# Moving the down-projection in front of the third score unit of its slot

## The chip, the cores and the metric

The kernel runs on one core of a Trainium2 chip. The metric is device time in microseconds (us) of one execution, taken as the median over several runs. The engines of the core run their own instruction lists side by side and wait for each other by semaphores: TensorE (PE, with its weight loads shown as PEld), VectorE (DVE), ScalarE (ACT), GpSimd (POOL) and SyncE (SP, which here only starts DMAs).

## The reference

Two parts follow each other. The first is an attention in which keys and values are a pooled and projected image; the second adds, to each row, the output of two out of eight small adapters.

```
kv_pool = kv averaged over 4 x 4 patches          # 4 images of 384 x 32 -> 768 rows of 128
k = v = kv_pool @ w_sr
s = q @ k.T / sqrt(128);  a = softmax(s);  x = a @ v        # 4 x 12288 queries
logits = x @ w_gate;  the two largest of 8 get softmax weights w, the rest 0
out = x + sum over e of w[e] * (x @ A[e]) @ B[e]            # A: 128 -> 16, B: 16 -> 128
```

The eight adapters together are one 128 x 128 matrix A (the down-projection) and one 128 x 128 matrix B (the up-projection); the weights w scale the 128 hidden values in between, 16 for each adapter.

## The kernel before

The 49152 query rows are cut into 96 chunks of 512. A loop runs over slots, and in each slot several chunks are at different stages:

- `unit()` takes the next score unit from a list: for one chunk and two of the six blocks of 128 keys, `scores` makes two matmuls of 512 columns into a PSUM tile `sg` (pool `ps_s`, two buffers), and ACT writes their exponential to `em`. Three units make a chunk, and there are three `unit()` calls in a slot.
- `attend(k, s)` makes six matmuls with `em` as weights into `acc`; four of them (s = 0 to 3) make the attention output of a chunk. `normalize` divides on DVE (`rinv`, then `xn`).
- `top` and `route` find the two adapters (DVE's MAX8 and then POOL), `tanhs` and `gates` make the weights `gw` (one ACT instruction and two on POOL).
- `transposes(x, h, engine)` turns, with TensorE, `xn` of one chunk and the gated hidden values `hg` of another into one PSUM tile `tt_ps`, which DVE copies to `tts` in SBUF. Some chunks have their `hg` turned by a DMA instead (`turn_h_dma`, to a tile `ht`), and the chunks from number 68 to 89 have both turned by DMA.
- `down(x)` makes four matmuls with the turned `xn` as weights into `h_ps`; `gate(x)` multiplies `h_ps` by `gw` on DVE to `hg` (or `hs`). `up(u)` makes four matmuls into `d_ps`; `finish(u)` adds `xn` on DVE (`osb`) and stores.

`tt_ps`, `h_ps`, `d_ps` and the tiles for preparing keys and values of the next image (`kpT_ps`, `v_ps`, `kfT_ps`) all come from the pool `ps_m` with two buffers, in the order in which they are asked for. `keep` fixes the program order on each engine, so the order in which the lines stand is the order in which each engine takes its instructions.

From slot 8 on the loop at line 588 writes the order. In a common slot it is: first `unit()` (line 600), `tanhs`, `normalize`, `transposes`, second `unit()` (653), `up` and `finish` (654 to 656), `attend(…, 0)` (663), `top` and `route` (665), then from slot 13 on the third `unit()` (667) and in slots 8 to 12 `attend(…, 1)` in its place (670), then `down` (673) and `gate` (675 or 681), then the rest of the `attend` calls. Slots whose chunks are all turned by DMA leave the loop earlier, at line 636. Where a piece of the preparation of the next image is due, it stands between `gate` and the last `attend` calls (line 684).

Of the kernel before, what the change touches and what calls it, by code (L numbers as in the profile page):

```python
# [20 lines left out]
def kernel(  # L21
# [47 lines left out]
    def mm(*a, **k):  # L69
        return keep(nc.tensor.matmul(*a, **k))  # L70

    def mtile(shape, dtype=FP32, name="mb"):
        return ps_m.tile(shape, dtype, tag="mb", name=name)
# [12 lines left out]
    def load_qT(g):  # L86
        if g < B * NG - GC:
            t = qpool.tile([P, GT], BF16, tag="qT", name="qT")
        else:
            if "q" not in spare:  # L90
                spare["q"] = kvpool.tile([P, 4, 2, 4 * C], FP32, tag="kvr", name="qTs")
            t = spare["q"][:, g % GC].rearrange("p x c -> p (x c)").bitcast(BF16)
        keep(nc.sync.dma_start(t.rearrange("c (i r) -> c i r", r=16), q_bf[g], transpose=True))
        qT[g] = t
# [228 lines left out]
    def normalize(k):  # L323
        ri = rpool.tile([P, S], FP32, tag="rinv", name="rinv")
        keep(nc.vector.reciprocal(ri, acc[k][:, :, VC]))  # L325
        k0, m = first[k], k - first[k]
        if m == 0:
            xg[k0] = ring[len(xg) % len(ring)]
        x = xg[k0][:, m]
        keep(nc.vector.tensor_tensor(x[:, :, 0:VC], acc[k][:, :, 0:VC],  # L330
                                     ri.unsqueeze(2).broadcast_to([P, S, VC]), op=ALU.mult))
        xn[k] = x
# [12 lines left out]
    def top(k):  # L345
        k0, m = first[k], k - first[k]
        if m == 0:
            srt[k0] = rpool.tile([P, GC, S, 8], FP32, tag="srt", name="srt")
        for s in range(S):
            keep(nc.vector.max(srt[k0][:, m, s], xn[k][:, s, C:C + E]))  # L350
# [3 lines left out]
    def route(k0):  # L354
        n = size[k0] * S
        eng = nc.gpsimd if k0 > 1 else nc.vector
        lg = xg[k0].rearrange("p m s c -> p (m s) c")[:, 0:n, C:C + E]
        so = srt[k0].rearrange("p m s e -> p (m s) e")[:, 0:n]

        def over(i):  # L360
            d = rpool.tile([P, GC * S, 8], FP32, tag=f"over{i}", name=f"over{i}")[:, 0:n]
            keep(eng.tensor_tensor(  # L362
                d, lg, so[:, :, i].unsqueeze(2).broadcast_to([P, n, 8]), op=ALU.subtract))
            return d

        arg, mask = over(0), over(1)
        keep(eng.tensor_tensor(arg, arg, mask, op=ALU.add))
        keep(eng.tensor_scalar(mask, mask, 0.0, None, op0=ALU.is_ge))  # L368


        later.append(lambda: gates(k0, n, eng, arg, mask))
# [40 lines left out]
    def narrow(k, t):  # L412
        keep(nc.gpsimd.tensor_copy(strip(t, 0)[:, 0], xn[k][:, :, 0:C]))
# [13 lines left out]
    def down(k):  # L427
        hp[k] = mtile([P, S, P], name="h_ps")
        for s in range(S):
            mm(hp[k][:, s], xT[k][:, s], a_bf, start=(s == 0), stop=(s == S - 1))  # L430
# [10 lines left out]
    def up(k):  # L441
        dp[k] = mtile([P, S, C], name="d_ps")
        for s in range(S):
            mm(dp[k][:, s], hgT[k][:, s], b_bf, start=(s == 0), stop=(s == S - 1))
# [30 lines left out]
    def unit(k=None, r=None):  # L475
        k, r = units.pop(0 if k is None else units.index((k, r)))
        scores(k, r)
# [26 lines left out]
    def begin(k, queries=True):  # L504
        nonlocal sums, rest
        b, i = divmod(k, NB)
        g = k // GC
        if k in loads and queries:
            load_qT(loads[k])
        if k in casts:  # L510
            cast_q(4 + casts.index(k))
        if k in rows_at:
            load_kv(*rows_at[k], None)
        if i == 0 and 0 < b < B - 1:
            rest = prepare(b + 1, nc.gpsimd)[1]
        if k == 3:
            sums, rest = prepare(1, nc.gpsimd)
            sums = sum(sums, [])
        if 3 <= k < 15:
            load_kv(1, (k - 3) // 4, (k - 3) % 4, None)  # L520
        if k == 7:
            for _ in range(2):
                sums.pop(0)()

    def tanhs():
        while later:
            later.pop(0)()
# [60 lines left out]
    for k in range(k1, NCHUNK):  # L588
        b, i = divmod(k, NB)
        ka = att.get(k, [])  # L590
        kx = enter.get(k, [])
        begin(k, False)

        def after_norm(kn):
            top(kn)
            if kn == first[kn] + size[kn] - 1:
                route(first[kn])

        kn = [n for n in att.get(k - 1, []) if normed[n] == k]
        unit()  # L600
        if k in loads and not any(x_ in by_queue for x_ in kx):
            load_qT(loads[k])
        ku = ku + late_up.pop(k, [])
        if kx and not kd and all(x_ in by_dma for x_ in kx):
            down(kx[0])
            todo = []
            for n in kn:
                normalize(n)
                if n in by_dma:
                    narrow(n, k)  # L610
                    todo = [(xT, n)]
            tanhs()
            for h_ in kh:
                if h_ not in by_dma:
                    transposes(None, h_, nc.vector)
            unit()
            gate(kx[0], strip(k, 0)[:, 1])
            todo.append((hgT, kx[0]))
            if len(kx) == 1:
                turn_dma(k, *todo)  # L620
            for u_ in ku:
                up(u_)
                finish(u_)
            attend(ka[0], 0)
            attend(ka[0], 1)
            unit()
            for n in kn:
                after_norm(n)
            attend(ka[0], 2)
            for x_ in kx[1:]:  # L630
                down(x_)
                gate(x_, strip(k, 0)[:, 0])
                turn_dma(k, (hgT, x_), *todo)
            attend(ka[0], 3)
            kh, ku = kx, [c for c in kh if c not in by_queue]
            continue
        tanhs()
        for x_ in kd:
            down(x_)
        for n in kn:  # L640
            normalize(n)
            if n in by_dma:
                narrow(n, k)
                turn_dma(k, (xT, n))
        px = [c for c in kx if c not in by_dma]
        ph = [c for c in kh if c not in by_dma and c not in by_queue]
        pairs = [(px[j] if j < len(px) else None, ph[j] if j < len(ph) else None)
                 for j in range(max(len(px), len(ph)))]
        for x_, h_ in pairs[:1]:
            transposes(x_, h_, nc.vector)  # L650
        for x_ in kd:
            gate(x_)
        unit()
        for u_ in ku:
            up(u_)
            finish(u_)
        for a_ in ka[:-1]:
            for s in range(S):
                attend(a_, s)
            normalize(a_)  # L660
            after_norm(a_)
        if ka and len(ka) == 1:
            attend(ka[0], 0)
        for n in kn:
            after_norm(n)
        if k >= 13:
            unit()
            n0 = 1
        else:
            attend(ka[0], 1)  # L670
            n0 = 2
        for x_ in kx[:1]:
            down(x_)
            if x_ in by_queue:
                gate(x_, hpool.tile([P, S, P], BF16, tag="hs", name="hs"))
                turn_h_dma(x_)
                late_up[k + 6] = [x_]
                if k in loads:
                    load_qT(loads[k])
            else:  # L680
                gate(x_)
        kd = []
        if rest and i in ((14, 15, 16, 18, 19, 20, 21, 22, 23) if b == 0 else (5, 6, 7, 13, 14, 15, 21, 22, 23)):
            rest.pop(0)()
        for a_ in ka[-1:]:
            for s in range(n0 if len(ka) == 1 else 0, S):
                if s == S - 1:
                    for x_, h_ in pairs[1:]:
                        transposes(x_, h_, nc.scalar)
                        kd = [x_] if x_ is not None else []  # L690
                attend(a_, s)
        ku = [c for c in kh if c not in by_queue]
        kh = kx[:1] + kdone
        kdone = kd
        if k % 2 == 0 and 8 <= k <= 20:
            for _ in range(4 if k == 18 else 3):
                sums.pop(0)()
        for w in adds_at.get(k, []):
            add_patches(*w)
# [181 lines left out]
```

## Time and profile before

| | us |
|---|---|
| median of 3 runs | 378.32 |
| the runs | 382.02, 377.99, 378.32 |
| profiled execution, its own time | 378.59 |
| its span (first to last instruction) | 376.8 |
| mean granted TensorE clock | 0.993 of full |

The profile lists for each engine how long it was busy, and in a timeline each instruction (equal neighbours merged, with their count) with its start, its duration, and in brackets the idle time ahead of it and what ended that. Matmuls overlap in it: a new one starts while the one before still runs out, and the ends are modelled. So TensorE's pace is read from the starts. PSUM and SBUF tiles carry the program's names; line 70 is the helper that records every matmul, so matmuls are told apart by their tiles.

### The profile page before, as it was taken

The numbers are of one execution on the slowest core, as the hardware profiler recorded it, in microseconds if no ns is written. First come the engines' busy times: TensorE is split into PE (matmuls) and PEld (weight loads), VectorE is DVE, ScalarE is ACT, GpSimd is POOL, SyncE is SP. The second block draws the span as 40 slices with busy tenths as digits, with TensorE's granted clock in tenths as the row PEclk, the third lists the DMA queues.
The fourth block names the chain that finished last, engine by engine and source line by source line (L and its number), as shares of the span: only waits on it lengthen the run. The fifth ranks groups of instructions, "written<-read, shape, count | busy, mean of one in ns | idle before, by whom it ended". The sixth has DMA issues, their size and how long they took to land.

```text
span 376.8 us, 11335 instructions
## 1 busy us (share of the span) xinstructions
PE 365.9 (97%) x4340; PEld 287.5 (76%) x4340; DVE 300.5 (80%) x925; ACT 293.6 (78%) x368; POOL 218.2 (58%) x493
## 2 busy tenths in 40 slices
PE   8899999999999999999999999999999999999993
PEld 5667788877788787877877787787877777777782
DVE  1446799888888888888888888898898777777785
ACT  1548986787878788788878868877878999999873
POOL 0120368888766566557557566755645666666452
PEclk9999999999999999999999999999999999999997
DMA  8979669999999999999999999999875686777523
GB/s 255 397 261 218 231 176 271 298 268 255 240 288 265 185 288 312 182 241 294 240 259 249 287 275 203 204 257 243 211 211 156 169 170 170 169 151 186 143 88 139
DMA packets 66311, 85.75 MB, mean 228 GB/s; under 512 B 42736, under 2 KB 43504, under 8 KB 65904
## 3 DMA queue, kind: packets, MB, share of 16 engines
q1 hardware_dynamic: 62656, 73.29, 70.0%
q0 software_dynamic: 3168, 11.54, 18.2%
q8 instruction: 34, 0.56, 0.6%
q10 hardware_dynamic: 432, 0.20, 0.2%
q14 instruction: 21, 0.17, 0.2%
HBM read 50.53 MB, written 36.70 MB: 232 GB/s over the span
## 4 chain that ended last, share of the span: by engine, by line
PE 88%; DMA 6%; DVE 3%; ACT 1%; issue 1%; POOL 0%; SPq 0%; ACTq 0%; POOLq 0%
PE acc L70 35%; PE sg L70 32%; PE tt_ps L70 6%; PE d_ps L70 5%; PE h_ps L70 5%; DMA kvr<-in_kv_dram 4%; DMA qf<-in_q_dram 2%; PE v_ps L70 1%; PE kpT_ps L70 1%; DVE xn L330 1%; DVE tts L399 1%; DMA out_dram<-osb 1%; ACT em L304 1%; PE kfT_ps L70 0%; PE tail_ps L70 0%
## 5 line engine op out<-in xcount | busy, mean ns | idle before, releaser
L304 ACT ACTIVATE em<-sg 128x1024 f16<-128x1024 f32 x288 | 282.7, 1022 | 64.7 <-PE sg L70 62.0
L70 PE MATMUL acc<-vx,em 128*128 128x136 f16 x2280 | 166.5, 223 | 0.0
L70 PEld LDWEIGHTS <-em 128*128 128x128 f16 x2304 | 145.3, 98 | 8.2 <-DVE xn L330 0.6
L70 PE MATMUL sg<-qT,kfT 128*128 128x512 bf16 x480 | 142.0, 379 | 0.8 <-ACT em L304 0.7
L330 DVE TENSOR_TENSOR xn<-acc,rinv 128x540 f32<-128x540 f32 x95 | 68.4, 720 | 3.3
L452 DVE TENSOR_TENSOR osb<-d_ps,xn 128x512 f32<-128x512 f32 x91 | 62.4, 688 | 1.1
L362 POOL TENSOR_TENSOR over<-xn,srt 128x64 f32<-128x64 f32 (+1 forms) x120 | 30.9, 278 | 50.5 <-DVE srt L350 50.4
L502 POOL TENSOR_TENSOR kvr<-kvr 128x512 f32<-128x512 f32 (+1 forms) x48 | 56.9, 1201 | 0.5
L70 PEld LDWEIGHTS <-tts 128*128 128x128 bf16 x456 | 34.6, 97 | 25.4 <-issue 0.4
L70 PEld LDWEIGHTS <-kfT 128*128 128x128 bf16 x576 | 46.3, 98 | 4.5 <-issue 1.0
L377 POOL TENSOR_TENSOR gw<-th,over 128x64 f32<-128x64 f32 (+1 forms) x60 | 17.3, 289 | 51.7 <-ACT th L375 49.6
L325 DVE RECIPROCAL rinv<-acc 128x4 f32<-128x4 f32 x95 | 17.3, 182 | 36.1 <-PE acc L70 35.2
L399 DVE COPY tts<-tt_ps 128x1024 bf16<-128x1024 bf16 (+1 forms) x73 | 41.6, 569 | 0.0
L435 DVE TENSOR_TENSOR hg<-h_ps,gw 128x512 bf16<-128x512 f32 x44 | 30.4, 691 | 9.1 <-POOL gw L378 8.4
L70 PEld LDWEIGHTS <-xn 128*128 128x128 bf16 x296 | 22.6, 98 | 16.7 <-DVE xn L330 0.4
L350 DVE MAX8 srt<-xn 128x8 f32<-128x8 f32 x380 | 34.5, 153 | 0.1
L70 PE MATMUL sg<-qTs,kfT 128*128 128x512 bf16 x96 | 28.6, 379 | 0.0
L70 PE MATMUL tt_ps<-id_bf,xn 128*128 128x128 bf16 x284 | 27.4, 219 | 0.0
L70 PE MATMUL h_ps<-a_bf,tts 128*128 128x128 bf16 x284 | 27.4, 219 | 0.0
L368 POOL TENSOR_SCALAR over<-over 128x64 f32<-128x64 f32 (+1 forms) x60 | 19.8, 331 | 5.3
L225 POOL TENSOR_TENSOR kvr<-kvr 128x512 f32<-128x512 f32 x18 | 22.5, 1271 | 0.1
L70 PEld LDWEIGHTS <-turn 128*128 128x128 bf16 x176 | 13.4, 98 | 10.2 <-issue 0.2
(97 smaller groups left out, 318.4 us busy)
## 6 DMA issues: line engine op xcount, KB each, us to landing
out_dram<-osb SPq DMA_DIRECT2D x94, 256.0 KB, 4.0
kvr<-in_kv_dram SPq DMA_DIRECT2D x45, 512.0 KB, 6.5
qbf<-in_q_dram POOLq DMA_DIRECT2D x22, 512.0 KB, 8.1
qf<-in_q_dram SPq DMA_DIRECT2D x8, 256.0 KB, 7.6
kvr<-in_kv_dram SPq DMA_DIRECT2D x6, 256.0 KB, 7.6
ht<-hs SPq DMA_TRANSPOSE x27, 6.6
out_dram<-osb SPq DMA_DIRECT2D x3, 128.0 KB, 2.4
turn<-turn SPq DMA_TRANSPOSE x23, 3.1
```

The costliest lines, as they stand in the source:

```text
L70: return keep(nc.tensor.matmul(*a, **k))
L225: keep(adder.tensor_tensor(u[:, lo:hi], u[:, lo:hi], v[:, lo:hi], op=ALU.add))
L304: keep(nc.scalar.activation(o, i_, AF.Exp, bias=0.0, scale=scale))
L325: keep(nc.vector.reciprocal(ri, acc[k][:, :, VC]))
L330: keep(nc.vector.tensor_tensor(x[:, :, 0:VC], acc[k][:, :, 0:VC], ri.unsqueeze(2).broadcast_to([P, S, VC]), op=ALU.mult))
L350: keep(nc.vector.max(srt[k0][:, m, s], xn[k][:, s, C:C + E]))
L362: keep(eng.tensor_tensor(d, lg, so[:, :, i].unsqueeze(2).broadcast_to([P, n, 8]), op=ALU.subtract))
L368: keep(eng.tensor_scalar(mask, mask, 0.0, None, op0=ALU.is_ge))
L399: keep(nc.vector.tensor_copy(sb[:, lo:hi], ps[:, lo:hi]))
L435: keep(nc.vector.tensor_tensor(hg[k].rearrange("p s (e r) -> p (s e) r", e=E), hp[k].rearrange("p s (e r) -> p (s e) r", e=E), gw[k0][:, m ...
L452: keep(nc.vector.tensor_tensor(osb, dp[k], xn[k][:, :, 0:C], op=ALU.add))
L502: keep(nc.gpsimd.tensor_tensor(u, u, v, op=ALU.add))
```

## The change

`down` for the first chunk that enters in a slot is called before the third `unit()` (or, in slots 8 to 12, before `attend(…, 1)`), directly behind the `after_norm` calls. `gate`, the DMA transpose and the load of further queries stay where they were.

```diff
         for n in kn:
             after_norm(n)
+        for x_ in kx[:1]:
+            down(x_)
         if k >= 13:
             unit()
             n0 = 1
...
             attend(ka[0], 1)
             n0 = 2
         for x_ in kx[:1]:
-            down(x_)
             if x_ in by_queue:
                 gate(x_, hpool.tile([P, S, P], BF16, tag="hs", name="hs"))
                 turn_h_dma(x_)
```

## The prediction

> **What bounds the kernel now.** I read the page first, then the waits, then the timeline of two slots in the middle, then the same places along the whole run.
>
> ```profile
> PE 365.9 (97%) x4340; PEld 287.5 (76%) x4340; DVE 300.5 (80%) x925; ACT 293.6 (78%) x368; POOL 218.2 (58%) x493
> ...
> PE 88%; DMA 6%; DVE 3%; ACT 1%; issue 1%; POOL 0%; SPq 0%; ACTq 0%; POOLq 0%
> ```
>
> ```profile
> ACT em L304 <- PE sg L70: 62.0, 80, 3.3
> ...
> PE sg L70 <- ACT em L304: 0.7, 1, 0.7
> ```
>
> TensorE carries 88% of the chain, and ACT waits 62.0 us for TensorE's scores while TensorE's own list has one wait of 0.7 us for ACT's exponentials. So TensorE's order and the holes in it decide. But "busy" overlaps from matmul to matmul: a row of four matmuls lasts 0.39 us although the next row starts 0.22 us later. A hole shorter than that overlap is not in the waits; it shows only in the distance between starts. One slot, then the next one (times of start and duration, in us):
>
> ```profile
> 151.83 0.59 PE L70 MATMUL sg<-qT,kfT 128*128 128x512 bf16 x2
> ...
> 152.52 1.02 ACT L304 ACTIVATE em<-sg 128x1024 f16<-128x1024 f32 x1 [0.75 <-PE sg L70]
> ...
> 152.89 0.41 DVE L399 COPY tts<-tt_ps 128x512 bf16<-128x512 bf16 x1
> ...
> 153.14 0.52 PE L70 MATMUL acc<-vx,em 128*128 128x136 f16 x6
> ...
> 153.60 0.59 PE L70 MATMUL sg<-qT,kfT 128*128 128x512 bf16 x2
> ...
> 154.03 0.39 PE L70 MATMUL h_ps<-a_bf,tts 128*128 128x128 bf16 x4
> ...
> 154.24 0.32 POOL L378 TENSOR_TENSOR gw<-gw,over 128x64 f32<-128x64 f32 x1
> 154.25 1.23 PE L70 MATMUL acc<-vx,em 128*128 128x136 f16 x18
> ...
> 154.59 0.69 DVE L435 TENSOR_TENSOR hg<-h_ps,gw 128x512 bf16<-128x512 f32 x1 [0.28 <-POOL gw L378]
> ...
> 155.31 0.59 PE L70 MATMUL sg<-qT,kfT 128*128 128x512 bf16 x2
> 155.51 0.18 DVE L325 RECIPROCAL rinv<-acc 128x4 f32<-128x4 f32 x1 [0.23 <-PE acc L70]
> ...
> 156.39 0.69 DVE L399 COPY tts<-tt_ps 128x1024 bf16<-128x1024 bf16 x1
> ...
> 156.85 0.52 PE L70 MATMUL acc<-vx,em 128*128 128x136 f16 x6
> ...
> 157.15 0.16 PEld L70 LDWEIGHTS <-kfT 128*128 128x128 bf16 x2
> 157.20 0.59 PE L70 MATMUL sg<-qT,kfT 128*128 128x512 bf16 x2
> ...
> 157.63 0.39 PE L70 MATMUL h_ps<-a_bf,tts 128*128 128x128 bf16 x4
> ...
> 157.89 0.41 PE L70 MATMUL kpT_ps<-id_f,kvr 128*128 128x128 f32 x2
> ```
>
> Call the first a light slot (one transposed tile: the copy tts is 512 wide) and the second a heavy one (two: 1024 wide). In the heavy slot six acc matmuls take 157.20 - 156.85 = 0.35 us. In the light slot the same six take 153.60 - 153.14 = 0.46 us: a hole of about 0.10 us in front of the third score unit. What ends it is in the rows: the scores of the third unit go into the PSUM buffer of the first (there are two), ACT's exponential of the first ends at 152.52 + 1.02 = 153.54, and the matmul starts 0.06 us later. From the first unit's start that release takes 153.60 - 151.83 = 1.77 us; TensorE has only 1.67 us of work to put in between. The heavy slot has four more transposes (0.22 us), arrives after the release and has no hole.
>
> I followed this distance through all slots: 30 have the hole, all between 72 and 280 us.
>
> ```profile
> 71.96 0.52 PE L70 MATMUL acc<-vx,em 128*128 128x136 f16 x6
> ...
> 72.41 0.59 PE L70 MATMUL sg<-qT,kfT 128*128 128x512 bf16 x2
> ```
>
> ```profile
> 278.53 0.52 PE L70 MATMUL acc<-vx,em 128*128 128x136 f16 x6
> ...
> 279.04 0.59 PE L70 MATMUL sg<-qT,kfT 128*128 128x512 bf16 x2
> ```
>
> These are the first (0.45 us) and the last (0.51, a hole of 0.16).
>
> **The change part by part.** The four matmuls of the down-projection (0.22 us, 154.03 to 154.25) are put in front of the third unit's two score matmuls. Nothing is added or removed. The move takes no DMA with it: gate, the DMA transpose behind it and load_qT stay, and the two programs' instruction lists differ on TensorE alone, so the order on DVE, ACT, POOL and SP is the old one. The slots that run all by DMA transposes take another path and are untouched.
>
> *The hole.* In a light slot the down-projection needs the copy tts, which ends at 152.89 + 0.41 = 153.30; TensorE gets there at 153.50 (153.14 + 0.35). It runs until 153.72, after the release, so the third unit no longer waits: the 0.10 us is filled. 27 slots at 0.10 and the last at 0.16: 2.9 us. (The other two holes are below.)
>
> *What becomes late.* The third unit's scores start 0.12 us later in a light slot and 0.22 us later in a heavy one. Only its exponential follows, and that stands in ACT's order behind two others, with ACT idle before the next slot's first exponential (the 0.75 us in the row at 152.52); I cost this at nothing. If that idle time were gone it would be 0.1 to 0.2 us a slot. The gate gets its input earlier, but in light slots it starts when POOL's gw is done (154.24 + 0.32 = 154.56, then 154.59), so it gains nothing and costs nothing. Behind it DVE has 0.23 us idle before the reciprocal; the slot's gain takes 0.10 of that, and the reciprocal is still released by TensorE.
>
> *The new wait.* The down-projection now waits for tts closer behind it. In the heavy slot tts ends at 156.39 + 0.69 = 157.08. How soon can a TensorE instruction follow a DVE copy for which it waits? Here is one that does, in a slot with two up-projections:
>
> ```profile
> 273.60 0.69 DVE L399 COPY tts<-tt_ps 128x1024 bf16<-128x1024 bf16 x1
> ...
> 274.25 1.29 DVE L452 TENSOR_TENSOR osb<-d_ps,xn 128x512 f32<-128x512 f32 x2
> 274.34 0.38 PE L70 MATMUL d_ps<-b_bf,ht 128*128 128x128 bf16 x4
> ...
> 274.92 0.59 PE L70 MATMUL sg<-qT,kfT 128*128 128x512 bf16 x2
> ```
>
> 0.05 us (274.34 - 274.29). So in the heavy slot the weights can be loaded from 157.08 + 0.05 = 157.13 on, and the place in the stream is 157.15, where the kfT load stands today. The margin is 0.02 us by rows that are rounded to 0.01 each, so somewhere from nothing to 0.04, and I found the same distance in every heavy slot. The whole chain from the reciprocal to tts hangs on TensorE's last acc matmul, so the margin moves with TensorE and does not shrink as slots get shorter. I count 33 places with it: the heavy slots, the light slot at 279, and five early slots without a third unit, where the down-projection goes in front of six acc matmuls instead:
>
> ```profile
> 52.23 0.69 DVE L399 COPY tts<-tt_ps 128x1024 bf16<-128x1024 bf16 x1
> ...
> 53.34 0.27 PEld L70 LDWEIGHTS <-tts 128*128 128x128 bf16 x4
> ```
>
> (ready at 52.97, and 53.34 - 0.35 = 52.99.) The cost is between nothing and, if each is met just late, 0.02 us: 0 to 0.7 us. I take 0.1, because the row with a true wait resumes at its full pace (four matmuls in 0.22 us).
>
> *Two slots without an up-projection* (no d_ps between the second unit and acc) reach the place before tts is ready:
>
> ```profile
> 75.43 0.69 DVE L399 COPY tts<-tt_ps 128x1024 bf16<-128x1024 bf16 x1
> ...
> 76.12 0.59 PE L70 MATMUL sg<-qT,kfT 128*128 128x512 bf16 x2
> ```
>
> ```profile
> 83.03 0.69 DVE L399 COPY tts<-tt_ps 128x1024 bf16<-128x1024 bf16 x1
> ...
> 83.66 0.59 PE L70 MATMUL sg<-qT,kfT 128*128 128x512 bf16 x2
> ```
>
> tts ends at 76.12; load at 76.17, matmul 0.05 later at 76.23 (the distance of the rows at 157.15 and 157.20). TensorE then stands where it stood at 76.12 before: 0.11 us lost. In the second, 83.72 + 0.05 + 0.05 = 83.82 against 83.66: 0.16 lost. Together 0.3 us.
>
> *Three slots with two up-projections* (at 274, 283 and 358): h_ps gets the PSUM buffer of the first d_ps, so it waits for the first osb. At 274.25 + 0.69 + 0.05 = 274.99 against 274.92 that is 0.07 each, 0.2 us.
>
> *A small gain.* Six slots load fp32 weights behind the down-projection: 157.63 + 0.22 = 157.85, and kpT_ps starts at 157.89. Behind a score matmul, which streams for 0.22 us alone, that load is hidden: about 0.03 each, 0.2 us.
>
> Sum: -2.9 + 0.1 + 0.3 + 0.2 - 0.2 = -2.5 us. The profiled execution took 378.59 us (span 376.8), so 376.1; it lies 0.3 above the median of 378.32, against which the forecast is **375.8 us**. All of the gain should reach the end, since behind 280 us TensorE runs to its tail without a wait for anything that this moves.
>
> **The rivals.** *The tight margin is missed and the weight load is laid bare.* Against it stand the 0.05 us and that the margin is the same everywhere. For it: 0.02 us is about the rounding of the rows that give it, and a load that waits can't be done under the matmul before it. Its price is one load:
>
> ```profile
> L70 PEld LDWEIGHTS <-tts 128*128 128x128 bf16 x456 | 34.6, 97 | 25.4 <-issue 0.4
> ```
>
> 33 x 0.097 = 3.2 us, in place of the 0.1: 376.1 + 3.1 = 379.2, by the median 378.9, slightly slower than before. It decides where the release takes over 0.07 us instead of 0.05. A rule of the Trainium skill speaks on this side: its page "TensorE: Matmul & The Clock Gate", Part 2, says that weight loads are pulled ahead of matmuls in flight, and gives a load as columns / 1.2, so an estimate of 107 ns for 128; a load held by its wait would lose that. The trace agrees on the load (97 ns), but the waiting row at 274.34 does not tell whether its load was bare. Chance 0.14, of which 0.08 for a cost of more than 0.19 us a place (6.3 us), which is what a loss of over 1% takes.
>
> *Something else is late at the new pace and the hole comes back elsewhere* (DMA, SP or POOL): the time stays at about 378.3. For it, POOL's gw stands 0.03 us ahead of every light gate. Against it, no wait of TensorE on DMA appears in the listed waits of the middle of the run, and only 0.1 us in two slots is asked of it. Chance 0.08.
>
> *More than the sum*: all 30 holes (3.1 us) and the fp32 loads go and nothing is lost: 378.3 - 3.3 = 375.0. To pass 1%, 3.8 us are needed, more than the holes hold. Chance 0.06 for over 1%.
>
> **How the numbers follow.** The forecast has the remaining 0.72, with its own range of 375.0 to 376.6. A difference of 1% (3.8 us) is about what a measurement of this kernel can tell from no change; the forecast's 0.7% lies within it. Within 1%: 0.72 + 0.08 + 0.06 = 0.86; faster 0.06; slower 0.08. The range from 374.9 to 378.5 takes in the no-change rival and leaves out the loss and a gain beyond the holes.
>
> **What would show it.** Right: in the timeline, six acc matmuls, then four h_ps at 0.35 us, then the score unit 0.22 us later in light and heavy slots alike; light slots shorter by 0.10 us (3.48 here, 155.31 - 151.83) and heavy ones unchanged. Wrong: heavy slots with more than 0.35 us between the six acc and h_ps, and a new wait of TensorE's weight load on DVE tts; or light slots as long as before.

## The result, and the profile after

The changed kernel took 376.22 us (median of 19 runs, 375.47 to 379.36), the kernel before beside it 378.94 us (19 runs, 377.99 to 382.58): a ratio of 0.9924, with an interval from 0.9902 to 0.9946. Run beside it again later, the ratio was 0.995 (0.992 to 0.998). The forecast was 375.8 us, 2.5 us less than before and under 1%; by the medians the gain is 2.7 us, or 0.7%. (Ratios leave out the few executions that lie more than 1.5% above the fastest of their kernel; medians hold all.)

The first lines are from the page of the changed kernel's profiled execution (375.47 us, span 373.7), the next from its list of waits (total us, times, longest):

```profile
PE 362.7 (97%) x4340; PEld 285.2 (76%) x4340; DVE 297.2 (80%) x925; ACT 296.7 (79%) x368; POOL 218.3 (58%) x493
...
PE 90%; DMA 3%; DVE 3%; ACT 2%; issue 1%; POOL 0%; SPq 0%; ACTq 0%; POOLq 0%
```

```profile
ACT em L304 <- PE sg L70: 52.3, 80, 3.2
...
PE sg L70 <- ACT em L304: 0.7, 1, 0.7
```

TensorE still carries the chain. ACT's wait for scores fell from 62.0 to 52.3 us; ACT has 1 to 2% of the chain, and this fall by 9.7 us is not the gain. The gain is read from the starts. A heavy slot and the light one behind it, in the changed kernel's timeline (start, duration):

```profile
146.76 0.59 PE L70 MATMUL sg<-qT,kfT 128*128 128x512 bf16 x2
...
147.84 0.69 DVE L399 COPY tts<-tt_ps 128x1024 bf16<-128x1024 bf16 x1
...
148.30 0.52 PE L70 MATMUL acc<-vx,em 128*128 128x136 f16 x6
...
148.59 0.27 PEld L70 LDWEIGHTS <-tts 128*128 128x128 bf16 x4
148.65 0.39 PE L70 MATMUL h_ps<-a_bf,tts 128*128 128x128 bf16 x4
...
148.88 0.59 PE L70 MATMUL sg<-qT,kfT 128*128 128x512 bf16 x2
...
150.37 0.59 PE L70 MATMUL sg<-qT,kfT 128*128 128x512 bf16 x2
...
151.06 1.02 ACT L304 ACTIVATE em<-sg 128x1024 f16<-128x1024 f32 x1 [0.53 <-PE sg L70]
...
151.68 0.52 PE L70 MATMUL acc<-vx,em 128*128 128x136 f16 x6
...
152.04 0.39 PE L70 MATMUL h_ps<-a_bf,tts 128*128 128x128 bf16 x4
...
152.26 0.59 PE L70 MATMUL sg<-qT,kfT 128*128 128x512 bf16 x2
...
153.13 0.69 DVE L435 TENSOR_TENSOR hg<-h_ps,gw 128x512 bf16<-128x512 f32 x1 [0.28 <-POOL gw L378]
...
153.76 0.59 PE L70 MATMUL sg<-qT,kfT 128*128 128x512 bf16 x2
```

In both slots h_ps follows 0.35 or 0.36 us behind the first of the six acc matmuls and the score unit 0.22 or 0.23 us behind h_ps. The light slot takes 153.76 - 150.37 = 3.39 us (3.48 before), the heavy one 150.37 - 146.76 = 3.61. That is as long as before, where the heavy slot ahead of the light one at 151.83 began at 148.22:

```profile
148.22 0.59 PE L70 MATMUL sg<-qT,kfT 128*128 128x512 bf16 x2
```

In the light slot the exponential ends at 152.08 and its buffer's next matmul starts at 152.26: the hole is filled. The gate still starts when POOL's gw is done, 2.76 us behind the slot's first score as before (154.59 - 151.83).

To compare whole executions I took the time from the first score matmul of slot 13 to the first matmul of the tail, called the stretch below: 296.90 us before (67.04 to 363.93), 294.40 after (66.43 to 360.83). That is 2.50 us less, the sum of the forecast. The remaining 0.6 of the 3.1 us between the spans lies ahead of slot 8, where the two kernels are the same: the five early slots in which `down` moves take 15.88 us in both (51.16 to 67.04 before, 50.55 to 66.43 after). Three executions of the changed kernel reached slot 13 at 65.96, 66.43 and 67.04 us, so one kernel differs by as much there. From the tail's first matmul to the end it takes 12.87 us before and 12.86 after.

### The profile page after: what moved, and what is told of

Its sections match the earlier page's. It is cut to its first block, busy times and chain, and to the rows that moved or that the text cites. A ratio compares the mean times of both kernels' runs of the same rounds, so it can differ in the third digit from the quotient of the medians.

```text
span 373.7 us, 11335 instructions
## 1 busy us (share of the span) xinstructions
PE 362.7 (97%) x4340; PEld 285.2 (76%) x4340; DVE 297.2 (80%) x925; ACT 296.7 (79%) x368; POOL 218.3 (58%) x493
## 4 chain that ended last, share of the span: by engine, by line
PE 90%; DMA 3%; DVE 3%; ACT 2%; issue 1%; POOL 0%; SPq 0%; ACTq 0%; POOLq 0%
PE acc L70 35%; PE sg L70 32%; PE tt_ps L70 6%; PE h_ps L70 6%; PE d_ps L70 5%; PE kpT_ps L70 2%; DMA kvr<-in_kv_dram 2%; PE v_ps L70 1%; ACT em L304 1%; DVE xn L330 1%; PE qT_ps L70 1%; PE kfT_ps L70 1%; DMA turn<-turn 1%; DMA out_dram<-osb 1%; DVE tts L399 0%
## 5 line engine op out<-in xcount | busy, mean ns | idle before, releaser
L304 ACT ACTIVATE em<-sg 128x1024 f16<-128x1024 f32 x288 | 285.8, 1022 | 58.1 <-PE sg L70 52.3
L70 PEld LDWEIGHTS <-em 128*128 128x128 f16 x2304 | 146.8, 98 | 16.5 <-DVE xn L330 0.6
L70 PEld LDWEIGHTS <-kfT 128*128 128x128 bf16 x576 | 45.0, 98 | 2.6 <-issue 1.0
L70 PEld LDWEIGHTS <-tts 128*128 128x128 bf16 x456 | 32.3, 98 | 11.1 <-issue 0.4
```

Source lines behind the costliest of these rows:

```text
L304: keep(nc.scalar.activation(o, i_, AF.Exp, bias=0.0, scale=scale))
```

## The experiments

Times are of the stretch in the profiled execution, unless they are medians; a ratio is to the kernel before, run beside it.

**The change in parts.** Three runs make the move only in some slots; elsewhere `down` stands where it stood before.

```diff
-        for x_ in kx[:1]:
+        for x_ in kx[:1] if early else []:
             down(x_)
...
         for x_ in kx[:1]:
+            if not early:
+                down(x_)
```

The first has `early = k >= 13 and not ph` (light slots only):

> The down-projection is moved in the light slots alone (one transposed tile, from slot 13 on); heavy slots and slots 8 to 12 stay as before. Theory (the gain is the filled hole in front of the third score unit): 27 light slots shorter by 0.10 us each, the hole at about 279 us and the two in slots without an up-projection stay; 2.75 us less than before, ratio 0.993. Rival (the gain comes from an earlier gate, anywhere): only part of the changed kernel's 2.7 us, about half, 0.9965.

294.25 us, 2.65 less than before; ratio 0.9977 (0.9946 to 1.0008). The second has `early = k < 13 or bool(ph)`, the rest of the moves:

> The down-projection is moved in the heavy slots and in slots 8 to 12 alone; light slots stay as before. Theory: no gain, as there is no hole to fill except at 279 us (0.16); two slots without an up-projection lose about 0.1 each and three slots with two of them 0.08 each: 0.3 us more than before, ratio 1.001. Rival (earlier gate, anywhere): about half of the gain, 0.9965. Rival (tight margin missed): 3 us slower, 1.008.

297.01 us, 0.11 more; ratio 1.0002 (0.9986 to 1.0017). Two rows from the timeline of the second, at a light slot where nothing was moved:

```profile
153.14 0.52 PE L70 MATMUL acc<-vx,em 128*128 128x136 f16 x6
...
153.60 0.59 PE L70 MATMUL sg<-qT,kfT 128*128 128x512 bf16 x2
```

The hole is there (0.46 us for six acc matmuls), in 27 slots, while heavy slots run without one. By the traces the whole gain comes from the light slots, and moving `down` in the heavy ones brings nothing; the two parts together give 2.54 us, the whole 2.50. The ratio of the light part alone shows less than its trace: 2.65 us would be 0.993, below its interval, which takes in 1. Waits for DMA as those below, which come and go from execution to execution, may make up the difference; its other executions left no trace to show it. The third run has `early = k >= 13 and len(ku) == 1`, which leaves out the slots with no up-projection, with two, and those ahead of slot 13:

> The down-projection is moved only in slots from 13 on that have exactly one up-projection; slots 8 to 12, the two slots without one and the three with two stay as before. Theory (those slots only cost): 0.2 us for the two and 0.25 us for the three less than the changed kernel, 2.95 us less than before, ratio 0.992. Rival (they cost nothing in the whole): as the changed kernel, 0.9935.

294.97 us, of which TensorE waits 0.89 for a chunk turned by DMA (below); without that 294.08, 0.32 less than the changed kernel, where the terms to be saved had been put at 0.45. Ratio 0.9941 (0.9913 to 0.9969).

**How wide is the margin of the copy tts?** Here `down` stands between the fifth and the sixth matmul of `attend(…, 0)`, 0.059 us sooner than in the changed kernel:

```diff
-    def attend(k, s):
+    def attend(k, s, ahead=None):
...
         for j in range(J):
+            if ahead is not None and j == J - 1:
+                down(ahead)
```

> As the changed kernel, but from slot 13 on the down-projection stands one acc matmul (0.06 us) further ahead, between the fifth and the sixth of the first attend call, so that the tight margin of the heavy slots is missed by 0.05 us. Theory (a miss costs what it is late by, and 0.01 us to resume): 0.06 us in each of 29 heavy slots and in the five slots with none or two up-projections, nothing in light slots: 2.1 us more than the changed kernel, 0.6 us less than before, ratio 0.9985. Rival (a missed wait also lays a weight load bare): 0.16 us each, 5.4 us more than the changed kernel, 2.7 more than before, ratio 1.007.

296.15 us, of which 1.31 are two waits for DMA (0.53 for a group of queries, 0.78 for the chunk below); without them 294.84, 0.44 more than the changed kernel. A heavy slot in its timeline:

```profile
147.74 0.69 DVE L401 COPY tts<-tt_ps 128x1024 bf16<-128x1024 bf16 x1
...
148.20 0.46 PE L70 MATMUL acc<-vx,em 128*128 128x136 f16 x5
148.49 0.23 PEld L70 LDWEIGHTS <-tts 128*128 128x128 bf16 x4
148.49 0.40 PE L70 MATMUL h_ps<-a_bf,tts 128*128 128x128 bf16 x4
148.72 0.22 PE L70 MATMUL acc<-vx,em 128*128 128x136 f16 x1
```

tts ends at 148.43, the load starts 0.05 us behind it at 148.49, and h_ps starts at 148.49 too. That is in time: five acc matmuls of 0.059 us from 148.20 leave TensorE free at 148.49. In all 29 heavy slots with one up-projection the load waits for tts in this way, and there the four matmuls of h_ps take 0.232 us instead of 0.223: 0.009 us lost in each. The five slots that wait in the changed kernel already (two without an up-projection, three with two) pay the whole 0.059 us. Both expectations were too dear for the heavy slots (0.06 and 0.16 each). A load that is late by its wait is not laid bare: its matmul starts 0.005 us behind the load's start, where in the changed kernel it starts 0.058 behind. So the load may slip by about 0.05 us before its matmul does. In the changed kernel's heavy slots the load starts 0.06 us behind the end of tts, against 0.052 here where it waits. The margin there was thus about 0.06 us (0.01 up to the load's place and 0.05 of slip), not 0.02.

**Far past the margin.** `down` in front of the whole `attend(…, 0)`:

```diff
+        ahead = k >= 13 and len(ka) == 1
+        for x_ in kx[:1] if ahead else []:
+            down(x_)
         if ka and len(ka) == 1:
             attend(ka[0], 0)
```

> As the changed kernel, but from slot 13 on the down-projection stands ahead of the whole first attend call (six acc matmuls, 0.355 us sooner), so that tts is late by 0.35 us in heavy slots and by 0.27 us in light ones. The run with one matmul sooner cost 0.01 us a miss, as the matmul starts 5 ns after its late weight load and not 55. Theory (a late copy costs its lateness beyond 0.05 us, and 0.01 to resume): 0.31 us in 29 heavy slots, 0.23 in 27 light ones, 0.36 more in five others: 17 us more than the changed kernel, 14.5 more than before. Rival (other work hides it, and the miss stays near nothing): within 2 us of the changed kernel.

392.18 us (one run), and 310.63 us in the stretch: 16.2 more than the changed kernel. A heavy slot, in its timeline:

```profile
153.91 0.69 DVE L399 COPY tts<-tt_ps 128x1024 bf16<-128x1024 bf16 x1
...
154.14 0.39 PE L70 MATMUL d_ps<-b_bf,ht 128*128 128x128 bf16 x4
154.66 0.23 PEld L70 LDWEIGHTS <-tts 128*128 128x128 bf16 x4 [0.30 <-DVE tts L399]
154.66 0.40 PE L70 MATMUL h_ps<-a_bf,tts 128*128 128x128 bf16 x4
154.89 0.52 PE L70 MATMUL acc<-vx,em 128*128 128x136 f16 x6
```

0.29 us lost in each of 29 heavy slots, 0.22 in 27 light ones, and h_ps takes 0.23 us once it goes. So a move by 0.35 us costs 0.29 in a heavy slot, all but the 0.06 of margin; the changed kernel stands on the free side of it.

**Another filling.** Is it the down-projection that counts, or any work between the second and the third unit? The kernel before, with the next `attend` in front of the third unit and `down` behind it, as it was:

```diff
-        if k >= 13:
+        if k >= 13 and len(ka) != 1:
             unit()
             n0 = 1
...
             attend(ka[0], 1)
             n0 = 2
+            if k >= 13:
+                unit()
```

> The down-projection stays behind the third score unit; instead the second attend call of the slot (six acc matmuls, 0.35 us) is put in front of that unit, in every slot from 13 on. Theory (anything that fills the hole will do): all 30 holes go, nothing waits for tts any sooner; 3.0 us less than before, ratio 0.992, in the trace no more than 0.06 us between neighbouring matmul starts of acc and sg. Rival (the down-projection's own place, or the earlier gate, brings the gain): no gain, 1.000.

293.60 us, 3.30 less than before and 0.8 less than the changed kernel; ratio 0.9945 (0.9919 to 0.9971). A light slot in its timeline:

```profile
151.73 0.87 PE L70 MATMUL acc<-vx,em 128*128 128x136 f16 x12
...
152.44 0.59 PE L70 MATMUL sg<-qT,kfT 128*128 128x512 bf16 x2
...
152.88 0.39 PE L70 MATMUL h_ps<-a_bf,tts 128*128 128x128 bf16 x4
```

Twelve acc matmuls in 0.71 us, without a hole. Six acc matmuls (0.35 us) fill it as the four of the down-projection do, and h_ps asks for tts later than before, so it does not wait. Work of two kinds has now filled the hole, so the place of `down` is not the point. The 0.25 us beyond the 3.05 of the holes come mostly from kpT_ps, which no longer waits (the term of the fp32 loads below). To that the next run adds that the second up-projection of a slot goes behind the first `attend`:

```diff
-        for u_ in ku:
+        for u_ in ku[:1]:
             up(u_)
             finish(u_)
...
             attend(ka[0], 0)
+        for u_ in ku[1:]:
+            up(u_)
+            finish(u_)
```

> The second attend call ahead of the third score unit in every slot from 13 on, the down-projection behind the unit as before; and where a slot has two up-projections, the second stands behind the first attend call instead of directly behind the first. Theory: the holes go (3.3 us, as the run with the attend call alone had), and so do three waits of 0.29 us of the second up-projection for the buffer that the copy tts frees: 4.2 us less than before, ratio 0.989, in the trace 0.06 us where d_ps follows d_ps with 0.35. Rival (the wait comes back behind it, at h_ps or the next tile): 3.3 us less, 0.9913.

294.08 us, of which 1.34 are the wait below; without it 292.74, 0.86 less. In its timeline the second up-projection no longer waits for its PSUM buffer:

```profile
270.00 0.39 PE L70 MATMUL d_ps<-b_bf,tts 128*128 128x128 bf16 x4
270.23 0.52 PE L70 MATMUL acc<-vx,em 128*128 128x136 f16 x6
...
270.58 0.39 PE L70 MATMUL d_ps<-b_bf,ht 128*128 128x128 bf16 x4
```

0.58 us from the first to the second up-projection with six acc matmuls (0.35) between them, against 0.52 with nothing between in the changed kernel (rows below). Median 374.87 us, ratio 0.992 (0.9883 to 0.9956).

**The changed kernel again**, since other runs had shown waits that no theory held:

> The changed kernel itself, on the same chip as the next two, for comparison: 2.5 us less than before, ratio 0.9935.

Median 376.56 us, ratio 0.995 (0.992 to 0.998), and 296.29 us in the stretch, 1.89 more than in the first execution, all of it at one place. From its timeline:

```profile
277.47 0.61 POOL L413 CAST turn<-xn 128x512 bf16<-128x512 f32 x1
...
279.67 1.97 SPq L417 DMA_TRANSPOSE turn<-turn  x1
...
285.27 0.40 PE L70 MATMUL h_ps<-a_bf,turn 128*128 128x128 bf16 x4 [1.73 <-DMA turn<-turn]
```

This is the first chunk whose `xn` a DMA turns. POOL has it ready at 278.08; SP issues the transpose at 279.67, coming from other work without a pause; it lands at 285.22, and TensorE has waited. I took two transposes of queries, which SP takes shortly before, for the cause, and moved their load ahead, in the changed kernel and in the fastest one:

```diff
-    loads.update({57: 20, 59: 21, 61: 22, 64: 18, 65: 23, 66: 19})
+    loads.update({57: 20, 59: 21, 61: 22, 63: 23, 64: 18, 66: 19})
```

> The changed kernel with one load of queries (group 23) issued at slot 63 instead of 65, so that SP's two query transposes no longer stand right before the first chunk that the DMA turns. Theory (SP's queue is behind because of these two transposes): no wait of TensorE over 0.1 us for the first chunk turned by DMA (around 280 to 286 us), the stretch from slot 13's first score matmul to the first tail_ps matmul 294.4 us as in the changed kernel's quiet execution, ratio to the kernel before 0.9925. Rival (the chunk's own transposes land late, whenever SP has issued them): a wait of 1 to 2 us is left there in about half of the executions, ratio about 0.995.

> Run e7 (first attend in front of the third score unit, second up-projection behind it) with the same load moved to slot 63. Theory: the stretch is 292.7 us, which is 4.2 us less than the kernel before (296.9), no wait for the first chunk turned by DMA, ratio 0.989. Rival: the wait of 1 to 2 us for that chunk stays, ratio 0.992 as for e7.

294.98 us with a wait of 0.62, and 294.05 with one of 1.31; ratios 0.9958 (0.9933 to 0.9982) and 0.993 (0.9904 to 0.9955). The wait stayed, and SP came to the transpose behind time in both. So moving that load does not remove the wait, and this theory falls. The rival, the transpose's own time, explains a part: from issue to landing it took 4.6 to 6.0 us in executions with the wait and 4.2 to 4.9 without (2.4 in one). The shares differ. In the execution above SP was 1.6 us late and the transpose took 5.55 us, 1.0 more than in the changed kernel's first execution; with the second up-projection behind the first `attend`, SP was only 0.3 us late and the transpose took 5.96. Each of the two kernels was then run and profiled once more:

> The kernel before, one look. Both theories: the stretch is 296.9 us and TensorE does not wait for the first chunk turned by DMA, which came 0.83 us ahead of its need in the profiled execution; if the transposes land up to 2 us later in some executions at the old pace too, a wait of up to 1.2 us shows here.

> The changed kernel, one look. The stretch is 294.4 us if the first chunk turned by DMA is in time, or 295 to 296.4 us with a wait of 0.6 to 2 us for it near 283 us; nothing else differs from the earlier executions by more than 0.1 us.

The kernel before took 299.64 us this time (381.38 as a whole), with the same wait: 2.1 us for the chunk turned by DMA, and 0.6 for a group of queries. The expectation had allowed at most 1.2. From its list of waits:

```profile
PEld L70 <- DMA turn<-turn: 2.9, 3, 2.4
PE h_ps L70 <- DMA turn<-turn: 1.9, 1, 1.9
PEld L70 <- DMA qT<-qbf: 0.7, 1, 0.7
```

The changed one took 294.33 (374.94 as a whole) without it. All executions beside each other (us; "SP ahead" is how long SP stood waiting for the data in front of the first turned chunk's transpose, "SP held" the time for which two earlier transposes of queries, the same two in each kernel, held SP; "TensorE waits" is read from the starts):

| kernel | stretch | TensorE waits for DMA | without | SP ahead | SP held |
|---|---|---|---|---|---|
| before | 296.90 | 0 | 296.90 | 2.2 | 11.8 |
| before, again | 299.64 | 2.73 | 296.91 | 0 | 20.9 |
| changed | 294.40 | 0 | 294.40 | 3.6 | 13.5 |
| changed, again | 296.29 | 1.89 | 294.40 | 0 | 18.6 |
| changed, third time | 294.33 | 0 | 294.33 | 1.5 | 11.6 |
| light only | 294.25 | 0 | 294.25 | 0.3 | 15.2 |
| heavy only | 297.01 | 0 | 297.01 | 1.9 | 12.3 |
| acc first | 293.60 | 0 | 293.60 | 2.1 | 12.9 |
| one matmul sooner | 296.15 | 1.31 | 294.84 | 0 | 21.4 |
| whole attend sooner | 310.63 | 0 | 310.63 | 1.6 | 21.5 |
| one up only | 294.97 | 0.89 | 294.08 | 0 | 17.4 |
| acc first, up later | 294.08 | 1.34 | 292.74 | 0 | 13.8 |
| changed, query load early | 294.98 | 0.62 | 294.36 | 0 | 15.8 |
| acc first, up later, load early | 294.05 | 1.31 | 292.74 | 0 | 17.4 |

Without the waits for DMA each kernel repeats to 0.1 us. And the wait is there exactly where SP came to that transpose with no time in hand: seven executions of seven, and in none of the other seven. Where SP lost the time is in the timeline of its queue, first of the kernel before and then of its second execution:

```profile
189.41 6.28 SPq L93 DMA_TRANSPOSE qT<-qbf  x1
...
204.47 5.51 SPq L93 DMA_TRANSPOSE qT<-qbf  x1
```

```profile
189.42 9.93 SPq L93 DMA_TRANSPOSE qT<-qbf  x1
...
207.54 11.00 SPq L93 DMA_TRANSPOSE qT<-qbf  x1
```

The same two instructions of the same kernel, the first issued at the same time to 0.01 us, hold SP's queue for 11.8 us in one execution and for 20.9 in the other. Over the executions the sum is 11.6 to 15.2 without the wait and 13.8 to 21.4 with it, so they mostly go together (the exception is "whole attend sooner": 21.5 it has no wait, but its TensorE is 16 us slower and may leave SP the time). That is a comparison of executions, not an experiment; why these transposes are sometimes slow, and whether a faster kernel makes it likelier, stays open.

The fastest version, acc first with the second up-projection behind the first `attend`, takes 292.74 us without the DMA waits, 4.2 less than before and 1.7 less than the changed kernel. Run side by side, its median lay 1.7 us below the changed kernel's (374.87 against 376.56); with the query load early in both, it lay 0.2 above (376.46 against 376.28). The ratios' intervals overlap, so only the traces tell the two apart.

## Why the prediction was right, point by point

**The hole** was as described. The 30 of it add up to 3.05 us by the starts, all are gone, and the 28 that the term holds (without the two slots with no up-projection) were worth 2.90, against 27 x 0.10 + 0.16 = 2.9. That the buffer's release ends it holds for each: in all 30 the score matmul starts 0.052 us behind the end of the exponential that empties its buffer, while no other score unit of that stretch starts less than 0.14 behind its own. That other work in the same place fills it as well (acc first) shows that it is nothing about `down`. What becomes late cost nothing, as forecast: ACT still has 0.53 us idle in the row at 151.06, where it had 0.75.

**The tight margin** cost nothing (0.1 was taken, 0 to 0.7 allowed). The reason given was too cautious: it measured to the place of the load, which can slip, and not to that of the matmul. One matmul sooner cost 0.009 us a slot. There were 29 heavy slots with this margin, two more than the 33 places hold; at no cost each, that changes nothing.

**The rival of the bare load** (+3.1 us) falls with it. The rule behind it, from the Trainium skill's page "TensorE: Matmul & The Clock Gate", Part 2, that loads are pulled ahead of matmuls in flight, agrees with the stream of the ordinary slots, in which a load starts 0.058 us ahead of its matmul. But that a load held by its wait would lose its estimated 107 ns, which I drew from it, the measurement contradicts: 0.005 us lie between the start of a late load and the start of its matmul.

**The slots without an up-projection** lose less than the 0.3 us. The first of them, in the changed kernel's timeline:

```profile
74.73 0.69 DVE L399 COPY tts<-tt_ps 128x1024 bf16<-128x1024 bf16 x1
...
74.96 0.52 PE L70 MATMUL acc<-vx,em 128*128 128x136 f16 x6
...
75.48 0.22 PEld L70 LDWEIGHTS <-tts 128*128 128x128 bf16 x4 [0.18 <-DVE tts L399]
75.48 0.40 PE L70 MATMUL h_ps<-a_bf,tts 128*128 128x128 bf16 x4
```

75.48 - 74.96 - 0.35 = 0.17 us of waiting, where the hole before was 0.10; in the other 0.16 against 0.04. Together 0.18, not 0.27: the step had added 0.05 us each from the late load to its matmul.

**The slots with two up-projections** wait as predicted, 0.08 us each (0.07 forecast), 0.24 in all. One in the changed kernel's timeline:

```profile
270.73 0.39 PE L70 MATMUL d_ps<-b_bf,tts 128*128 128x128 bf16 x4
...
271.16 1.29 DVE L452 TENSOR_TENSOR osb<-d_ps,xn 128x512 f32<-128x512 f32 x2
271.25 0.38 PE L70 MATMUL d_ps<-b_bf,ht 128*128 128x128 bf16 x4
...
271.47 0.52 PE L70 MATMUL acc<-vx,em 128*128 128x136 f16 x6
...
271.90 0.38 PE L70 MATMUL h_ps<-a_bf,tts 128*128 128x128 bf16 x4
```

The first of the two osb ends at 271.16 + 0.69 = 271.85 (0.69 is one of them, in the row at 155.49 below), and h_ps starts at 271.90 instead of 271.47 + 0.35 = 271.82. "One up only", which leaves both kinds of slots alone, wins back 0.32 of their 0.42.

**The small gain from fp32 loads** did not come where it was put. The rows for it, first of the kernel before, then of the changed one:

```profile
157.05 0.69 DVE L452 TENSOR_TENSOR osb<-d_ps,xn 128x512 f32<-128x512 f32 x1
```

```profile
155.49 0.69 DVE L452 TENSOR_TENSOR osb<-d_ps,xn 128x512 f32<-128x512 f32 x1
...
155.87 0.59 PE L70 MATMUL sg<-qT,kfT 128*128 128x512 bf16 x2
...
156.30 0.20 PEld L70 LDWEIGHTS kpT_ps<-id_f,kvr 128*128 128x128 f32 x2 [0.33 <-issue]
156.33 0.41 PE L70 MATMUL kpT_ps<-id_f,kvr 128*128 128x128 f32 x2
```

The scores end their place at 156.30 (0.43 behind 155.87) and kpT_ps still starts 0.03 late. Its PSUM buffer is that of d_ps, and osb, which empties it, ends at 156.18. From there to kpT_ps it is 0.15 us, and so it was before (osb ends at 157.74, kpT_ps starts at 157.89 in the prediction's row), though another matmul stood in front. So the 0.03 belong to that wait and not to the load. "Acc first", in which osb ends 0.47 us ahead of kpT_ps, has lost them. In return nine v_ps matmuls behind the same place, also with fp32 weights, became 0.17 us faster in all (0.056 us of delay each before, 0.042 after, none in the first), and the kpT_ps together lost about 0.04. So the term was -0.13 instead of -0.2, for another reason.

By the starts: -2.90 + 0 + 0.18 + 0.24 - 0.13 = -2.61, and +0.11 in small differences spread over the run: -2.50. The main term was right by its mechanism. That the sum is met so closely is partly luck: the terms that were off by about 0.1 cancelled.

**Something else late at the new pace** was given 0.08 for giving all back. The DMA did give back 1.9 us in one of the three profiled executions of the changed kernel; but the kernel before has it too (2.1 us in one of two), so it does not need the change. Whether the change makes it likelier is not shown. The sentence that TensorE runs to its tail without a wait behind 280 us held for the execution that was shown, and not for every one.

## What to carry to other kernels

Read TensorE's pace from the distances between starts: 30 holes of 0.10 us were 0.8% of the time and in no list of waits. A hole that a buffer's release makes can be filled with work whose inputs are long there; prefer work that waits for nothing new (the acc matmuls here) to work whose input has just been copied. And look at several executions before pricing the cover of a DMA: the one profile showed 0.83 us in hand (landed 285.13, first used at 285.96), the next execution of the same kernel a wait of 2.1.

## What was not expected of the hardware

A matmul whose weight load waited for tts starts 0.005 us behind the start of that load, where in the full stream of the changed kernel it starts 0.058 us behind, and the four of h_ps then take 0.23 us. A DMA transpose of queries, the same instruction in the same place, held SP's queue for 4.9 to 12.6 us (second of the pair, in "light only" and "one matmul sooner"). In the two executions of the kernel before, SP reached the first turn some 75 us later, at 278.39 and, where the pair had held it longer, at 284.06; that the one brought the other is likely but was not tested.
